# A memory-attention and spatial-gating kernel whose steps are issued in two newly written orders

## The chip, the cores and the metric

The kernel runs on one core of a Trainium2 chip. The time is in device microseconds (us), from the start of the program on the chip to its end; the median of several runs is compared. A profiled execution gives in addition the span of its instructions and, row by row, when each instruction of each engine began and how long it took. The engines of the core are TensorE (PE in the profile; its weight loads are PEld), VectorE (DVE), ScalarE (ACT), GpSimd (POOL) and SyncE (SP, which issues the transfers).

## The reference

Eight batches, eight heads, 576 positions of 64 numbers per head, 32 memories; the model is 512 wide, the hidden layer 1024.

```
# attention through 32 memories
a = softmax of phi over the 576 positions          # (8, 8, 576, 32)
k_m = einsum('bhsm,bhsd->bhmd', a, k)              # keys of the memories
v_m = einsum('bhsm,bhsd->bhmd', a, v)
attn = softmax(q @ k_m^T / 8, over the 32 memories)
x = attn @ v_m                                     # (8, 576, 512) with the heads side by side
# gated layer
h = relu(x @ w_in)                                 # w_in 512 x 1024
u, v = h[..., :512], h[..., 512:]
v_n = (v - mean(v)) / sqrt(var(v) + 1e-6)          # over the last axis
v_s = einsum('ts,bsd->btd', w_spatial, v_n) + b_spatial[None, :, None]
out = (u * v_s) @ w_out                            # w_out 512 x 512
```

w_in and w_out reach the chip as 64-bit floats; all else is float32.

## The kernel before

**The work.** Each batch passes through nine kinds of steps, each named by a letter.

- P: phi of one batch is loaded, its maximum over the positions taken (maxima `half` and `mx`, L319 to L325 on VectorE; a transpose through TensorE to `mt`, L341 on VectorE, and back to `mb`), subtracted (L349) and the exponential taken (ScalarE); then its sums `es` (again L319 to L325, on GpSimd unless the list `ON_VECTOR` names them).
- K: k and v are loaded; TensorE forms the memories' keys and values (L375), the sums give `den` (L397, L398), and small transposes give `kT` and `vT`.
- Q: q is loaded and transposed (batch 0 on TensorE, the others on VectorE).
- S: scores on TensorE, four transposes by VectorE into `sm` (L503), then the softmax over the memories: L509 (maximum), L512 (subtraction), an exponential on ScalarE, L517 (sum), L519 and L520 (reciprocal), L522 (product). After transposes to `aT` the result is split in a high part `ah` (ScalarE) and a low part `al` (L543).
- M0, M1: v_m times the two halves of w_in, so that x itself is never formed; split in `mh` and `ml` (L166).
- V0 to V4: for 128 positions each, the v half (L591), its relu, mean and variance and normalized form, split in `vh` and `vl` (L618).
- U0 to U3: 128 columns each of the u half (L640).
- G0 to G3: the spatial mixture of 128 columns into `ps` (L678), the product `g` of u and `ps` (L689 on VectorE), split in `gh` and `gl` for the first 512 positions and in `grh` and `grl` for the last 64 (casts on ScalarE, L702 on VectorE).
- O0 to O3: 128 positions of the output (`po`, L718). The first half of each reads `gh` and `gl` of two products g, the second half of the other two. O4 does the last 64 positions of two batches at once.

Large products are made of three TensorE products (high by high, high by low, low by high).

**The weights.** Further letters prepare the weights, once. D loads w_in in eight pieces of 512 KB (`raw`, L178). E and L decode the two halves of its columns from 64-bit words to `win_sb`: for each of two row halves, L187 and L193 (VectorE, exponent and fraction), L203, L205 and L208 (ScalarE), L210 (VectorE), then an addition (L216 on GpSimd or L218 on VectorE) and a multiplication (L226 on GpSimd or L223 on VectorE). `ON_VECTOR` says which of them VectorE takes. X0 to X3 do the same for w_out (`raw_out`), and split it in `woh` and `wol` (L251). W loads w_spatial (`w_sb`, `w_rem`) and the bias (`b_sb`); T0 to T4 transpose w_spatial on TensorE and split it in `wth` and `wtl` (L166, where VectorE does it).

**What sets the order.** Each step is a generator, and each token of a text advances one of them by one part. The text `START` runs the preparation and batch 0; the text `PLAN` is run for each of batches 1 to 7. A token `G2` advances the step G2 of the current batch, `S'` the scores of the next batch, `P''` the phi step of the one after it, and `*3` repeats the token. The schedule is manual for all five engines: on each, the instructions stand in the order in which the tokens issued them, and an engine waits at each instruction for its inputs and buffers, with all that stands behind. Waits between engines are worked out from the data; a buffer that is used again makes its next writer wait for its last reader.

```
        for kind, n, ahead in tokens(START):
            step(kind, n, ahead)
        for b in range(1, B):
            for at, (kind, n, ahead) in enumerate(steps):      # steps = the tokens of PLAN
                key = kind, n, b + ahead
                while b + ahead < B and done.get(key, 0) < upto[at]:
                    step(*key)
```

Of the kernel before, what the change touches and what calls it, by code (L numbers as in the profile page):

```python
# [23 lines left out]


START = """
    P*6 W D0 P*4 T1 P D1 B D1 E0 T2*2 D0 T2 D0 P*3 L0 T2 P T1 L0 T1 T2 L0 D0 L1 E0 T1 L0 T1 L1*2
    K E0*2 L0 T1 T2 L1 E0 K W*2 E0 L0 Q E0 T2 W L1 D1 T0 W D1 K E0 T1 K L1 T4 L0 L1 K L1 K Q K
    L0 K*2 T0 E1 T4 E1 T4 K*3 Q P' T4 Q K' Q*6 P'*2 Q*2 S K' E1 S P' S T0 P' T4 S P' M0 E1 T4 S
    E1 P'*2 S T4 M0 X0 M0 E1 T0*3 P' M0 T3 S M0 S P' T3 E1 M0 E1 P' M0 T3 M1 S*2 X1 T0 M1*2 T3  # L30
    P' M1 K' S T3 P' S*2 M1 S P'*2 Q' S T3 M1 K' S Q' U1 M1 T3 S K' U0 S K' X0 K'*2 S K' X1 K'
    X0*3 X1 X0 X1*2 V0 V1 X1 U1 V1 U0 V3 X0 B K' V0 X0 U1 X1*2 V1 U2 X1 U0 X1 V0 U3 X1 X0 P'' X0
    V1 Q'*2 U2 V3 V0 V2 K' Q' V1 X2 V1 V0 V3 V1 X0 U3 U2 V0*2 Q' V2*2 U3 V4*2 G0 P'' V3 V4 G1 S'
    V3 V2*2 S' V4 S' V3 S' G1 S' V2*2 V4 X3 V4 V3 V4 G0 M1' M0'*2 X2 G1 P'' V4 G0 M1' M0' P'' G1
    M0' M1' X2 X3 M1' X3 X2 K'' X2*2 P'' M0' G1 G0*2 M1' P'' M1' X2 G3 X3 G1 G2 P'' M0' X2 G3 X3
    G0 S' P'' G0 X3 G2 S' G3 G1*3 X2 M0' M1' G2 S' G3 X3*3 G2 X2 G0*2 P'' G3 G2 G3 Q'' P'' X2 X3
    G2 S' O1 O0 G3 G2 O3 P'' S'*3 X3 G3 O2 O1 O0 S' G2 O1 K'' O3 O1 O2 S'*2 O0 S' P'' O3 G2 O0
    S'*3 O3 G3 O2 P'' O2 P''*2
"""

PLAN = """
    U0 P'*3 K' P' V1 V0 U0 K' U0 K' V2 U2 V0 V1*3 U1 V2 V0 V2 V0 V4 U1 V1 V0 V2 K' Q' P'' V1 U1
    V3 U3 Q' U2 V1 V4*2 K' V2 P'' K'*2 P'' V3 P'' K' P'' V3 V4 K' K'' U3 K' S' U2 U3 V2 V4 S' V3
    S' V3 S'*2 G0 V4 G1 P'' M0' Q'' P'' M1' M0' S' V3 V2 S' M1'*2 G0 V4 G1 G0 V3 S' G1 V4 G0 P''
    M1' S' M0' Q G1 G0 M1' G0 S' G1 S' M1' K'' P'' G0 S' Q'' G1 G0*2 M0' G2 G3 P'' G2 S' G3 G1*3
    G2 G3 G2*3 M1' G3 O3 G2 S' G3 S'*2 O0 G3 S' O1 G3 O0 S' G3 P'' M0' S' O3 O0 G2 O0 G3 O1 O3
    M0' O3 O4 G2 Q'' O2 M0' O1 O4 O1 V0' O2 O4*2 Q'' O2 V0' O2
"""

ON_VECTOR = set(  # L50
# [760 lines left out]
```

## Time and profile before

| | |
|---|---|
| median of 3 runs | 432.1 us (431.6 to 432.11) |
| span of the profiled execution | 429.2 us |
| TensorE, products | 399.7 us busy (93%), 3844 instructions |
| TensorE, weight loads | 335.9 us (78%) |
| VectorE | 292.5 us (68%), 536 |
| ScalarE | 228.3 us (53%), 438 |
| GpSimd | 81.7 us (19%), 154 |
| transfers | 50.69 MB, 118 GB/s on average |
| costliest lines of the chain that ended last | L678 29%, L718 23%, L591 14%, L640 12%, all TensorE |

The profiled execution's time is its span and what lies around it; the median of the runs is 2.9 us above that span. The page cuts the span in 40 slices of 10.7 us. TensorE's busy digits begin with 3176799 and are 9 from the sixth slice to the last but one; TensorE's clock is at 9 tenths or more in all slices but the fifth, where it is 6. So two stretches can be told apart: a head of some 50 us, in which weights arrive and are decoded, and a long stretch in which TensorE is always busy. In rows of single instructions, the first number is the start in us, the second the duration; then come engine, line, operation, output and inputs with partitions x elements and type, and in brackets how long the engine had idled just before and what ended that. For a group of rows that are alike (x2), the start is that of the first, and the duration covers the group.

### The profile page before, as it was taken

What the parts mean: (1) busy time and instruction counts of PE and PEld (TensorE: products, weight loads), DVE (VectorE), ACT (ScalarE), POOL (GpSimd) and SP (SyncE); (2) the same over time, 40 slices, a digit from 0 to 9 for tenths busy, and PEclk for the clock granted to TensorE, in tenths of its full rate; (3) what the DMA queues carried; (4) which work ended last, traced back from release to release, by engine and by line L of the source; (5) the groups of instructions that cost most, each with busy time, mean ns of one, the idle gap of its engine ahead of it and who ended that gap; (6) DMA issues with size and microseconds to landing.
All of it is one profiled execution on the core that took longest, in us unless ns stands there. A gap on an engine that the chain in (4) does not pass through costs nothing.

```text
span 429.2 us, 9278 instructions
## 1 busy us (share of the span) xinstructions
PE 399.7 (93%) x3844; PEld 335.9 (78%) x3844; DVE 292.5 (68%) x536; ACT 228.3 (53%) x438; POOL 81.7 (19%) x154
## 2 busy tenths in 40 slices
PE   3176799999999999999999999999999999999996
PEld 2063487988798887988798887988798888988984
DVE  3699999994997358953897168955897069824420
ACT  2657697654845277245835176245825276337422
POOL 1344353332300031023200030003200040005000
PEclk9999699999999999999999999999999999999999
DMA  8989639217960369014941279025911200020003
GB/s 291 401 296 323 78 99 225 108 48 178 224 93 25 100 197 185 8 73 141 240 34 43 83 210 178 0 76 185 199 30 58 67 2 0 2 98 2 0 2 121
DMA packets 85790, 50.69 MB, mean 118 GB/s; under 512 B 66226, under 2 KB 70322, under 8 KB 85748
## 3 DMA queue, kind: packets, MB, share of 16 engines
q1 hardware_dynamic: 85748, 50.10, 45.3%
q8 instruction: 30, 0.49, 0.5%
q14 instruction: 12, 0.10, 0.1%
HBM read 40.65 MB, written 9.44 MB: 117 GB/s over the span
## 4 chain that ended last, share of the span: by engine, by line
PE 89%; DVE 4%; DMA 3%; ACT 2%; issue 1%; SPq 0%; ACTq 0%; DVEq 0%
PE ps L678 29%; PE po L718 23%; PE pv L591 14%; PE pu L640 12%; PE kvm L375 4%; PE mp L561 4%; PE sc L492 2%; DMA raw<-in_moe_w_in_dram 2%; DMA w_rem<-in_moe_w_spatial_dram 2%; DVE win_sb L218 1%; DVE power L210 1%; DVE sm L512 1%; ACT raw L208 1%; ACT qT L445 0%; DVE g L689 0%
## 5 line engine op out<-in xcount | busy, mean ns | idle before, releaser
L598 DVE BATCH_NORM_STATS2 st<-vr 128x6 f32<-128x512 f32 (+1 forms) x40 | 27.4, 686 | 46.6 <-ACT vr L595 46.6
L678 PE MATMUL ps<-wth,vh 128*128 128x288 f32 x256 | 57.8, 307 | 0.1
L603 POOL TENSOR_SCALAR rs<-mv 128x1 f32<-128x1 f32 (+1 forms) x40 | 11.6, 291 | 236.1 <-DVE mv L600 232.1
L700 ACT CAST gh<-g 128x512 fp32r<-128x512 f32 x32 | 19.9, 621 | 67.9 <-DVE g L689 67.9
L678 PE MATMUL ps<-wtl,vh 128*128 128x288 f32 x256 | 54.9, 296 | 0.0
L678 PE MATMUL ps<-wth,vl 128*128 128x288 f32 x256 | 54.7, 295 | 0.0
L718 PE MATMUL po<-woh,gh 128*128 128x512 f32 x128 | 50.5, 394 | 0.0
L718 PE MATMUL po<-wol,gh 128*128 128x512 f32 x128 | 50.4, 394 | 0.0
L718 PE MATMUL po<-woh,gl 128*128 128x512 f32 x128 | 50.3, 393 | 0.0
L678 PEld LDWEIGHTS ps<-wth,vh 128*128 128x128 f32 x256 | 40.6, 188 | 11.0 <-issue 5.5
L724 ACT COPY o<-po 128x512 f32<-128x512 f32 x36 | 21.1, 587 | 51.5 <-PE po L718 51.5
L678 PEld LDWEIGHTS ps<-wtl,vh 128*128 128x128 f32 x256 | 41.3, 188 | 0.0
L678 PEld LDWEIGHTS ps<-wth,vl 128*128 128x128 f32 x256 | 41.3, 188 | 0.0
L613 ACT ACTIVATE vr<-vr,sh,rs 128x512 f32<-128x512 f32 (+1 forms) x40 | 32.4, 815 | 2.6 <-POOL sh L608 2.3
L591 PE MATMUL pv<-mh,ah 128*128 128x512 f32 (+1 forms) x80 | 32.9, 411 | 0.0
L649 ACT ACTIVATE u<-pu 128x576 f32<-128x576 f32 x32 | 20.2, 659 | 21.8 <-PE pu L640 21.5
L595 ACT ACTIVATE vr<-pv 128x512 f32<-128x512 f32 (+1 forms) x40 | 23.8, 595 | 14.6 <-PE pv L591 14.6
L591 PE MATMUL pv<-ml,ah 128*128 128x512 f32 (+1 forms) x80 | 31.6, 395 | 0.0
L591 PE MATMUL pv<-mh,al 128*128 128x512 f32 (+1 forms) x80 | 31.6, 395 | 0.0
L689 DVE TENSOR_TENSOR g<-u,ps 128x576 f32<-128x576 f32 x32 | 23.9, 750 | 10.8 <-PE ps L678 10.5
L718 PEld LDWEIGHTS po<-woh,gl 128*128 128x128 f32 x128 | 24.0, 188 | 5.7
L718 PEld LDWEIGHTS po<-woh,gh 128*128 128x128 f32 x128 | 24.0, 188 | 5.2
(150 smaller groups left out, 872.2 us busy)
## 6 DMA issues: line engine op xcount, KB each, us to landing
kv_sb<-in_k_dram SPq DMA_DIRECT2D x8, 1152.0 KB, 6.9
kv_sb<-in_v_dram SPq DMA_DIRECT2D x8, 1152.0 KB, 8.9
out_dram<-o SPq DMA_DIRECT2D x32, 256.0 KB, 2.0
q_sb<-in_q_dram SPq DMA_DIRECT2D x28, 288.0 KB, 6.5
phi_sb<-in_phi_dram SPq DMA_DIRECT2D x8, 576.0 KB, 4.1
raw<-in_moe_w_in_dram SPq DMA_DIRECT2D x8, 512.0 KB, 8.1
raw_out<-in_moe_w_out_dram SPq DMA_DIRECT2D x4, 512.0 KB, 3.6
w_sb<-in_moe_w_spatial_dram SPq DMA_DIRECT2D x1, 1152.0 KB, 6.8
```

Source lines behind the costliest of these rows:

```text
L375: nc.tensor.matmul(kvm[r][32 * j : 32 * j + 32], phi_sb[halves[r], j, i, :], kv_sb[halves[r], j, :, i * D : (i + 1) * D], start=(i == 0), ...
L591: nc.tensor.matmul(pv, x[:, r, cs], m[:, r, DM:DFF], start=(n == 0), stop=(n == 5))
L595: nc.scalar.activation(vr, pv, AF.Relu)
L598: nc.vector.bn_stats(st6, vr)
L613: nc.scalar.activation(vr, vr, AF.Identity, bias=sh, scale=rs)
L640: nc.tensor.matmul(pu[:, hf, 0:HALF], m[:, r, cs], a[:, r, hf * HALF : (hf + 1) * HALF], start=(n == 0), stop=(n == 5),)
L649: nc.scalar.activation(u[:, dt, :].rearrange("p (a s) -> p a s", a=2), pu[:, :, 0:HALF], AF.Relu)
L678: nc.tensor.matmul(ps[:, hf, 0:HALF], a, w[:, hf * HALF : (hf + 1) * HALF], start=(n == 0), stop=(n == len(ops) - 1),)
L689: nc.vector.tensor_tensor(g.rearrange("p (a s) -> p a s", a=2), u[:, dt, :].rearrange("p (a s) -> p a s", a=2), ps[:, :, 0:HALF], op=ALU.mult,
L700: nc.scalar.copy(hi, x)
L718: nc.tensor.matmul(po, a, w, start=(n == 0), stop=(n == 11))
L724: nc.scalar.copy(o, po)
```

## The change

The texts `START` and `PLAN` are written anew. All steps, their operations, the shapes, the buffers and `ON_VECTOR` stay. Of the diff two lines of each text tell the form; what moves on the engines is shown below.

```
 START = """
-    P*6 W D0 P*4 T1 P D1 B D1 E0 T2*2 D0 T2 D0 P*3 L0 T2 P T1 L0 T1 T2 L0 D0 L1 E0 T1 L0 T1 L1*2
+    P D0 P*3 D0 P D1 P*2 D1 P*2 L0 P L0*2 W L0 T2 L0 P D0 T1 W D0 L0 T1 L0 Q L0 E0 T2 L1 E0 K*2
...
 PLAN = """
-    U0 P'*3 K' P' V1 V0 U0 K' U0 K' V2 U2 V0 V1*3 U1 V2 V0 V2 V0 V4 U1 V1 V0 V2 K' Q' P'' V1 U1
+    U2 P' V1 V0*2 U0 P' V1 P' V1 U2 V0 V1 V2 U2 V1 V4 V0*2 K' P' V1 K' V2 U0 K' V1 U3 Q K' V4 V2
...
```

**Loads at the start.** SyncE issues the transfers in this order from the start of the program; here is that piece as a difference, - before and + now.

```order
 L330 DMA phi_sb<-in_phi_dram 128x4x288
+L178 DMA raw<-in_moe_w_in_dram 128x1024 x4
 L260 DMA w_sb<-in_moe_w_spatial_dram 128x4x576
 L261 DMA w_rem<-in_moe_w_spatial_dram 64x576
 L263 DMA b_sb<-in_moe_b_spatial_dram 1x576 x2
-L178 DMA raw<-in_moe_w_in_dram 128x1024 x6
+L178 DMA raw<-in_moe_w_in_dram 128x1024 x2
+L434 DMA q_all<-in_q_dram 128x4x576
 L363 DMA kv_sb<-in_k_dram 128x4x576
 L363 DMA kv_sb<-in_v_dram 128x4x576
-L434 DMA q_all<-in_q_dram 128x4x576
 L178 DMA raw<-in_moe_w_in_dram 128x1024 x2
```

Four pieces of w_in now come directly behind phi and ahead of w_spatial, two more behind it, and q ahead of k and v; the last two pieces stay last.

**GpSimd in the head.** GpSimd's rows from the clearing of the bias buffer to the last decoding of w_in, as a difference; `es` are the sums of batch 0's phi, and the rows L216 and L226 decode w_in in halves of a tile.

```order
 L134 MEMSET t_90 64x512
 L259 MEMSET b_sb 64x576
+L226 TENSOR_TENSOR win_sb<-win_sb,power 128x512 x2
 L319 TENSOR_TENSOR half<-phi_sb 128x512
 L321 TENSOR_TENSOR half<-half 128x4x64
 L323 TENSOR_TENSOR es<-half 128x128
 L325 TENSOR_TENSOR es<-es,phi_sb 128x128
-L226 TENSOR_TENSOR win_sb<-win_sb,power 128x512 x2
 L216 TENSOR_TENSOR win_sb<-win_sb,raw 128x512 x2
 L226 TENSOR_TENSOR win_sb<-win_sb,power 128x512 x2
```

The first multiplication moves ahead of the sums; the order of the rest stays.

**VectorE at the scores of batch 0.** `sm` takes the four score transposes, `mx` and `half` are the maxima of batch 1's phi, and L210 joins sign and exponent of weights still to be decoded. Before:

```order
L319 TENSOR_TENSOR half<-phi_sb 128x512
L321 TENSOR_TENSOR half<-half 128x4x64
L503 STREAM_TRANSPOSE sm<-sc_0_0_361 128x288
L323 TENSOR_TENSOR mx<-half 128x128
L503 STREAM_TRANSPOSE sm<-sc_0_1_362 128x288
L325 TENSOR_TENSOR mx<-mx,phi_sb 128x128
L503 STREAM_TRANSPOSE sm<-sc_1_0_363 128x288
L503 STREAM_TRANSPOSE sm<-sc_1_1_364 128x288
L341 TENSOR_REDUCE cm<-mt_391 128x2
L509 TENSOR_REDUCE rmx<-sm 128x36
L210 SCALAR_TENSOR_TENSOR power<-raw,power 128x1024
```

And now, at the same place:

```order
L503 STREAM_TRANSPOSE sm<-sc_0_1_347 128x288
L193 TENSOR_SCALAR raw_out<-raw_out 128x512
L210 SCALAR_TENSOR_TENSOR power<-raw,power 128x1024
L319 TENSOR_TENSOR half<-phi_sb 128x512
L321 TENSOR_TENSOR half<-half 128x4x64
L323 TENSOR_TENSOR mx<-half 128x128
L325 TENSOR_TENSOR mx<-mx,phi_sb 128x128
L503 STREAM_TRANSPOSE sm<-sc_1_0_348 128x288
L503 STREAM_TRANSPOSE sm<-sc_1_1_349 128x288
L341 TENSOR_REDUCE cm<-mt_418 128x2
L509 TENSOR_REDUCE rmx<-sm 128x36
```

The decoding of the last w_in rows (L210) and the first of w_out (`raw_out`) moved ahead of the maxima, which now stand in one block between the second and the third score transpose, where they had alternated with the first three.

**VectorE around the fourth product g of batch 0.** `mp` are the products with w_in for batch 1 and `ml` their low parts; `rsum` and the second `sm` belong to the softmax of batch 1, and `phi_sb` with `mb` to phi of batch 2. Before:

```order
L166 TENSOR_TENSOR ml<-mp_0_1_870,mh 128x512
L166 TENSOR_TENSOR ml<-mp_1_1_860,mh 128x512
L210 SCALAR_TENSOR_TENSOR power<-raw_out,power 128x512
L702 TENSOR_TENSOR grl<-g,grh 128x64
L689 TENSOR_TENSOR g<-u,ps_3_938 128x576
L689 TENSOR_TENSOR g<-u,ps_2_947 128x576
L349 TENSOR_TENSOR phi_sb<-phi_sb,mb_1025 128x1152
L517 TENSOR_REDUCE rsum<-sm 128x36
L702 TENSOR_TENSOR gl<-g,gh 128x512 x2
L519 TENSOR_SCALAR rsum<-rsum 128x36
L520 RECIPROCAL rsum<-rsum 128x36
L522 TENSOR_TENSOR sm<-sm,rsum 128x1152
```

And now:

```order
L517 TENSOR_REDUCE rsum<-sm 128x36
L689 TENSOR_TENSOR g<-u,ps_3_946 128x576
L349 TENSOR_TENSOR phi_sb<-phi_sb,mb_960 128x1152
L519 TENSOR_SCALAR rsum<-rsum 128x36
L520 RECIPROCAL rsum<-rsum 128x36
L166 TENSOR_TENSOR ml<-mp_0_1_868,mh 128x512
L166 TENSOR_TENSOR ml<-mp_1_1_854,mh 128x512
L522 TENSOR_TENSOR sm<-sm,rsum 128x1152
L702 TENSOR_TENSOR gl<-g,gh 128x512
L702 TENSOR_TENSOR grl<-g,grh 128x64
L689 TENSOR_TENSOR g<-u,ps_2_988 128x576
```

The row L689 that reads `ps_2` makes the fourth product. The subtraction L349, the softmax rows L517, L519, L520 and L522 and one `gl` stood behind it and now stand ahead of it.

More of the change, by code (lines that the diff above doesn't have):

```diff
@@ L26 @@
 START = """
-    P*6 W D0 P*4 T1 P D1 B D1 E0 T2*2 D0 T2 D0 P*3 L0 T2 P T1 L0 T1 T2 L0 D0 L1 E0 T1 L0 T1 L1*2
[L28 to L38, printed above, removed]
+    P D0 P*3 D0 P D1 P*2 D1 P*2 L0 P L0*2 W L0 T2 L0 P D0 T1 W D0 L0 T1 L0 Q L0 E0 T2 L1 E0 K*2
@@ new lines @@
+    E0 P Q D1 E0 D1 L1 Q T2 L1 Q L1 E0*2 Q*2 T1*2 Q L1 P T2 P L1 Q P Q E0 T1 E0 Q T2 Q L1 X0 X1
+    L1 K W Q K T1 K E1 B E1 K T2 K*3 X0 T1 K P' K E1 K K' S X0 S X1 S E1*2 X1 T3 Q' T3 X1 M0 T3
+    E1 T2 P' M0 X1 P' M0 T3 P' T0 P' T0 S P' E1 S T3 P' M0 W T3 S T0*2 K' P' T3 P' M0*2 T0 S*2 P'
+    S E1 S X0 S X0*2 W T0 M1 P' M1 Q' M0 S*2 M1*2 P' M1 S T0 K' P' S T4 M1 P' S*2 P' X0 U0 M1 T4
+    S*2 K' T4 V0 K'*2 X0 V0*2 B K' X0 T4 U0 P'' V1 U0 U2 X1 Q' X1 K'*2 U2 V1 U2 V1 V2 V0 Q' V1 K'
+    V4 V0 Q' X0 U1 T4 P'' V0 P'' U1 X1 V0 V1 X1 X0 K' V4 V3 Q' K' V4 U1 U3 V2 U3 V1*2 V2 V4 X1 V3
@@ L39 @@
+    U3 X1 P'' S'*2 V4 X2 T4 V2 P'' G0 V3 T4 S' V2 G1 G0 P'' V3 V4 V2 S' V3 X2 M1' S' V3 P'' M0'
+    X2*2 M1' V2 X3 M0' M1' V3 X2*2 S' G1 M0' X3 V4 X3 V4 X2 G0 G1 P'' M0' G0 G1 G0 M0' X3 G0 M1'
+    G1 M1' S' G3*2 G1 P'' M1' K'' X3*2 X2 G1 M0' G1 G3 S' G1 G3 X3 G0 G2 O3 S' G2 X2 G3 G2 P'' X2
+    S' M0' G3 X3 Q'' M1' S' X3 P'' G0 X3 G2 O1 G3 X2 G0 G2 S' X3 G2 O0 S' G2 O2 S' G2 O1*2 O2*2
+    G2 O1 P'' K'' S' P'' O0 S' G3 P''*2 O0 O3 S' O0 S' O3 O2 S' O3 G3
 """
 PLAN = """
-    U0 P'*3 K' P' V1 V0 U0 K' U0 K' V2 U2 V0 V1*3 U1 V2 V0 V2 V0 V4 U1 V1 V0 V2 K' Q' P'' V1 U1
@@ L43 @@
[L43 to L47, printed above, removed]
+    U2 P' V1 V0*2 U0 P' V1 P' V1 U2 V0 V1 V2 U2 V1 V4 V0*2 K' P' V1 K' V2 U0 K' V1 U3 Q K' V4 V2
@@ L48 @@
+    Q' U3 V4 U0 U3 V3 U1 V2 K' U1 V2 V4 Q' K'*2 G0 K'*2 V3*2 K' S' V3 S' V4 S' U1 G0 V2 S' V4 G1
+    K'' S' P'' S' V3 S' K'' M0' V3 M0' M1' V2 M1' V4 G1 G0 P'' G1 S' V4 M1' V3 P'' G1*2 G0 M0' G2
+    M1' G2*3 G1 M1' G0 G3 G0 S' P''*2 G3 S' Q'' G3 S' G0 G1 G0 G3 G1*2 G0 S' M0' G2 O0 S' G2 M0'
+    G3 S' O1 M0' G2 G3 M0' M1' G3 S' P'' O1 P'' O0 S' O1 O2 M1' P'' S'*2 G2*2 O2 P'' O2 G3 P'' O1
+    Q'' O4 O0 O2 O3 G3 O4*2 S' O0 O4 O3 Q''*2 P'' V0' O3*2 V0'
 """
```

## The prediction

> **What bounds the kernel now.** I read the page's first two parts, then busy time by stretch, then the rows of each engine in order of time.
>
> ```profile
> PE 399.7 (93%) x3844; PEld 335.9 (78%) x3844; DVE 292.5 (68%) x536; ACT 228.3 (53%) x438; POOL 81.7 (19%) x154
> 10.00:20.00 10.00, 2.11 (x6) 0.95 (x4) 5.61 (x8) 6.21 (x10) 3.57 (x4) 1.00 1.04 403
> 41.10:44.30 3.20, 0.00 (x0) 0.00 (x0) 3.20 (x3) 1.65 (x3) 3.20 (x3) 0.94 0.90 114
> 44.30:47.10 2.80, 2.68 (x17) 0.51 (x17) 2.73 (x4) 1.64 (x3) 2.09 (x2) 0.50 1.07 139
> 47.30:50.70 3.40, 2.92 (x81) 2.22 (x81) 3.31 (x9) 2.57 (x6) 0.00 (x0) 0.50 0.66 57
> 52.50:90.80 38.30, 38.28 (x289) 32.82 (x284) 35.72 (x68) 29.42 (x56) 18.42 (x23) 1.00 0.49 121
> 90.80:425.30 334.50, 334.38 (x3111) 286.03 (x3109) 216.74 (x413) 167.22 (x321) 44.94 (x109) 1.00 0.39 92
> ```
>
> In the rows by stretch the columns are the stretch, its length, busy time of PE, PEld, DVE, ACT and POOL, the granted clock, the DMA share and GB/s. From 52.5 us TensorE does not pause: 38.28 of 38.30 us, then 334.38 of 334.50. Before that it idles. So the time is TensorE's fixed work plus what it idles in the head, and a new order of the steady part can only lose there. Until 90.8 VectorE is nearly as full (35.72 of 38.30), so it is the engine to account for.
>
> One place allows an exact comparison.
>
> ```profile
> 85.92 1.40 DVE L689 TENSOR_TENSOR g<-u,ps 128x576 f32<-128x576 f32 x2
> 86.69 0.62 ACT L700 CAST gh<-g 128x512 fp32r<-128x512 f32 x1 [1.47 <-DVE g L689]
> 90.80 0.39 PE L718 MATMUL po<-woh,gh 128*128 128x512 f32 x1
> ```
>
> The row at 90.80 is the 25th projection matmul of batch 0, the first that reads the second half of gh. The two orders have the same matmuls ahead of it (all of K0, K1, M0, M1, V0, U0, S1, G0 and the first halves of O0 to O3) and the same behind it. Behind it TensorE has 334.5 us of work without a pause, in either order, unless the new steady part stalls. The change is therefore worth (start of this matmul in the new order) − 90.80. It needs the fourth product g (here ending at 87.32) and its cast.
>
> **The new order's transfers.** phi lands at 4.83 (first DVE row below). Then come 2.10 MB of w_in, 1.33 of w_spatial, 1.05 of w_in, and 1.18 each of q, k and v: 8.0 MB at 403 GB/s (row of 10 to 20 us) is 19.9 us, so v lands near 24.7. TensorE's memories K0 began at 24.64 in this profile, held by transposes of w_spatial. So K0 does not move; q now lands first, its transposes fill TensorE's idle time, and scores can follow K0 at about 30.3 instead of 34.0. That 3.7 us is the change's real gain.
>
> **VectorE against GpSimd.** The gain has to pass VectorE, and its rows beside GpSimd's decoding are long.
>
> ```profile
> 27.77 4.41 POOL L226 TENSOR_TENSOR win_sb<-win_sb,power 128x512 f32<-128x512 f32 x2 [12.83 <-DVE win_sb L218]
> 24.07 1.22 DVE L223 TENSOR_TENSOR win_sb<-win_sb,power 128x1024 f32<-128x1024 f32 x1
> 29.08 1.96 DVE L223 TENSOR_TENSOR win_sb<-win_sb,power 128x1024 f32<-128x1024 f32 x1
> 30.96 1.76 DVE L187 TENSOR_SCALAR power<-raw 128x1024 int32<-128x1024 int32 x1
> 37.88 3.51 POOL L216 TENSOR_TENSOR win_sb<-win_sb,raw 128x512 f32<-128x512 f32 x2 [5.71 <-ACT raw L208]
> 38.52 1.73 DVE L210 SCALAR_TENSOR_TENSOR power<-raw,power 128x1024 int32<-128x1024 int32 x1
> 40.17 2.44 DVE L512 TENSOR_TENSOR sm<-sm,rmx 128x1152 f32<-128x1152 f32 x1
> 41.36 3.62 POOL L226 TENSOR_TENSOR win_sb<-win_sb,power 128x512 f32<-128x512 f32 x2
> 45.23 1.28 DVE L519 TENSOR_SCALAR rsum<-rsum 128x36 f32<-128x36 f32 x1
> 78.99 1.34 DVE L509 TENSOR_REDUCE rmx<-sm 128x36 f32<-128x1152 f32 x1
> 80.67 1.44 POOL L216 TENSOR_TENSOR raw_out<-raw_out 128x512 f32<-128x512 f32 x1 [0.34 <-ACT raw_out L208]
> 80.85 2.47 DVE L512 TENSOR_TENSOR sm<-sm,rmx 128x1152 f32<-128x1152 f32 x1
> ```
>
> L223 takes 1.22 us alone and 1.96 beside GpSimd, and ends when GpSimd's first multiplication (27.77, half of 4.41) has ended plus 1.1 of its own. L512 takes 2.44 and 2.47 beside GpSimd; without it the equally large L522 takes 1.36 (below), a wait of 1.1. Reductions (L509, 1.34) don't wait. The reading that fits them all: an operation of VectorE with two SBUF inputs, or a TENSOR_SCALAR from SBUF, and one of GpSimd take turns, each waiting for the other's whole instruction. In this profile the waits ahead of the fourth g come to about 6.2: 0.74 (L223), 1.1 (L187), 0.5 (L210), 1.1 (L519), 1.1 twice (L512), 0.6 at 12 to 15 us.
>
> The new order puts four short dependent operations (the maxima of phi, L319 to L325) straight beside GpSimd's four half-tiles of the last w_in decoding.
>
> ```profile
> 33.86 0.67 DVE L319 TENSOR_TENSOR half<-phi_sb 128x512 f32<-128x512 f32 x1
> 34.56 0.42 DVE L321 TENSOR_TENSOR half<-half 128x256 f32<-128x256 f32 x1
> 36.16 0.25 DVE L325 TENSOR_TENSOR mx<-mx,phi_sb 128x128 f32<-128x128 f32 x1
> 36.33 0.84 DVE L503 STREAM_TRANSPOSE sm<-sc 128x288 f32<-128x288 f32 x2
> 50.94 0.76 DVE L543 TENSOR_TENSOR al<-aT,ah 128x576 fp32r<-128x576 f32 x1 [0.29 <-ACT ah L541]
> ```
>
> By my sum GpSimd starts L216 at 33.7 (ScalarE's L203, L205 and L208 behind den), VectorE L319 at 33.8. All four lose a turn of 1.1 us: 1.7 becomes 6.2, so L325 ends near 40 and the last two score transposes behind it begin at 40.1 rather than near 35.6; here they began at 36.33. The rest of the softmax (L509, L512, exp, L517, L522, transposes, ah, al) follows at 11.3 us, so the first al ends at 51.4, against 51.70 here. The 3.7 us are gone. A milder case: where VectorE's next instruction is already due, GpSimd waits (row at 56.71, below), L319 then escapes, and the four waits are three.
>
> ```profile
> 56.71 2.22 POOL L226 TENSOR_TENSOR raw_out<-raw_out,power 128x512 f32<-128x512 f32 x1 [10.24 <-issue]
> 57.10 0.68 DVE L218 SCALAR_TENSOR_TENSOR raw_out<-raw_out 128x512 f32<-128x512 f32 x1
> ```
>
> The Trainium skill, page "SBUF — State Buffer", section "Who interferes with whom", says that whichever of the two issues first holds the shared ports for its whole instruction and the other fully blocks. By it L216, 0.1 us ahead, keeps all four waits; by the row just shown it is three, and the sum would be 1.1 us lower.
>
> **What stands ahead of the fourth g.** Counted over the rows of the two orders, five VectorE operations of batch 1's softmax, one of phi, and one gl move ahead of it; nothing moves behind.
>
> ```profile
> 87.24 1.34 DVE L349 TENSOR_TENSOR phi_sb<-phi_sb,mb 128x1152 f32<-128x1152 f32 x1
> 88.51 1.34 DVE L517 TENSOR_REDUCE rsum<-sm 128x36 f32<-128x1152 f32 x1
> 89.77 1.28 DVE L702 TENSOR_TENSOR gl<-g,gh 128x512 fp32r<-128x512 f32 x2
> 91.17 0.38 DVE L520 RECIPROCAL rsum<-rsum 128x36 f32<-128x36 f32 x1
> 91.59 1.36 DVE L522 TENSOR_TENSOR sm<-sm,rsum 128x1152 f32<-128x1152 f32 x1
> ```
>
> By start-to-start distance: L349 1.26, L517 1.26, one gl 0.6, L519 and L520 0.5, L522 1.26: +4.9 us.
>
> Waits for GpSimd ahead of it in the new order: 2.4 at 15 to 21 (L187, two L193, L210 beside the sums of phi, L319 to L325 on GpSimd), 4.5 at 33 to 40, then about 1.1 each for L321 beside L251, L210 beside L216, a grl beside the second L216, and a gl beside L251, and 0.7 in small ones: 12.0, so +5.8.
>
> VectorE's own idling falls.
>
> ```profile
> 4.83 0.69 DVE L319 TENSOR_TENSOR half<-phi_sb 128x512 f32<-128x512 f32 x1 [4.83 <-DMA phi_sb<-in_phi_dram]
> 8.44 1.35 DVE L349 TENSOR_TENSOR phi_sb<-phi_sb,mb 128x1152 f32<-128x1152 f32 x1 [0.90 <-PE mb L347]
> 12.65 1.98 DVE L187 TENSOR_SCALAR power<-raw 128x1024 int32<-128x1024 int32 x2 [2.85 <-DMA raw<-in_moe_w_in_dram]
> 16.45 0.69 DVE L187 TENSOR_SCALAR power<-raw 128x1024 int32<-128x1024 int32 x1 [0.96 <-DMA raw<-in_moe_w_in_dram]
> 19.67 2.36 DVE L210 SCALAR_TENSOR_TENSOR power<-raw,power 128x1024 int32<-128x1024 int32 x2 [0.73 <-ACT power L205]
> 22.81 1.23 DVE L218 SCALAR_TENSOR_TENSOR win_sb<-win_sb,raw 128x1024 f32<-128x1024 f32 x1 [0.77 <-ACT raw L208]
> ```
>
> With w_in behind phi, 0.90 + 2.85 + 0.96 + 0.73 + 0.77 = 6.2 us of idling go, and one of 2.9 comes (the third pair of w_in now lands behind w_spatial, near 15.8). About 1.2 us of waits under 0.6 go as well, since VectorE is late: −4.5. Six more dependent operations in direct succession lose some 0.1 each: +0.6.
>
> Fourth g: 87.32 + 4.9 + 5.8 − 4.5 + 0.6 = 94.1 (93.0 with three waits). Cast and hand-over, 0.03 + 0.62 + 0.1 (row at 86.69): the 25th matmul at 94.9.
>
> **The clock.** Here TensorE did nothing from 41.1 to 44.3, and its clock was 0.50 until 50.7. In the new order it has nothing from about 36.2 to 40.6 (its next row waits for the maxima), and little until 43.5. I expect a half-clock stretch again, but with TensorE's K1, T4, U0 and V0 in it, which VectorE waits for. What it adds lies between 0 (no stretch, or over by 47) and 3.0 (until 54); I take 1.2, nearer to its end at 50.7 as here. The Trainium skill, "TensorE: Matmul & The Clock Gate", section on the HAM clock gate, gives a window of 3.4 us without work to halve the clock and one of busy work to restore it; this profile's 3.2 us agree, and by its free-running window the end could fall anywhere from 50.7 to 54.
>
> Sum: 96.1 − 90.80 = +5.3. The profiled span is 429.2, the median of the runs 432.1, so 2.9 lie around it; I add the difference to the median: 437.3, rounded to 437.2.
>
> **TensorE's own floor.** Without any wait for g, TensorE would reach the 25th matmul at about 90.7: the first U0 starts near 51.1 instead of 52.5, but 1.3 us of K1 are then still to do. So VectorE's lateness counts in full from there.
>
> **Costed at nothing.** The steady order: every instruction stays, and by the rows' durations no matmul waits over 0.25 us; VectorE's slack there (216.74 busy of 334.5) covers it. If that cover failed by 0.2 us a batch, seven batches would add 1.4. The SP queue's reordered loads have landed 10 us or more before use.
>
> **Rivals.**
> - The turns fall the other way, GpSimd giving way to VectorE as at 57.10, everywhere. Then 4.5 + 5.1 of the waits vanish, al ends near 47, TensorE runs from there and is ahead: about −3.2, 428.9, faster. It decides if L321 to L325 run at their bare 0.3 to 0.4. Against it: L223, L512 (twice) and L519 all waited. 8%.
> - TensorE hides VectorE's lateness: the fourth g ends before 90. That needs 4 of the 6.8 us to be misjudged. 432.1. 7%.
> - Worse: half clock until 54 and all four waits, or a stall in each steady batch: +6.5 to +8.5, near 439.6. 12%.
> - The forecast, 434 to 439: 73%.
>
> No change that can be told is within 0.2% (0.9 us). Faster 0.09 (the first rival and a little of the second), same 0.06, slower 0.85. The range leaves out the first rival, half of the second and the end of the third: 432.4 to 440.4.
>
> **What will show it.** Right: L321, L323 and L325 near 35 to 40 us at 1.2 to 1.6 each; the last two L503 at about 40; clock 0.50 between 40 and 51 or later; the fourth g near 94 to 96; TensorE waiting for L689 or L700 between 76 and 97, some 4 us in all. Wrong: short maxima rows, the 25th projection matmul near 91 or earlier, or pauses of TensorE behind it.

## The result, and the profile after

The changed kernel takes 437.09 us (median of 4 runs, 436.02 to 437.62) against 432.11 of the kernel before: a ratio of 1.012, with a 95% interval of 1.0103 to 1.0136. The forecast was 437.2. As the account below shows, the sum came out right because wrong terms of it cancelled.

The profiled execution has a span of 435.5 us, 6.3 more than the one before; the medians differ by 5.0. Executions of the kernel before with a span of 429.2 took 431.0 us, so its profiled execution was 1.1 us faster than its median, and that much of the 6.3 is scatter.

The busy times on the page of the changed kernel:

```profile
PE 399.1 (92%) x3844; PEld 334.6 (77%) x3844; DVE 292.7 (67%) x536; ACT 229.3 (53%) x438; POOL 73.4 (17%) x154
```

Stretches of the changed kernel, as in the prediction (start and end, length, busy time of PE, PEld, DVE, ACT and POOL, clock, DMA share, GB/s):

```profile
5.00:10.00 5.00, 0.92 (x2) 0.36 (x2) 3.25 (x7) 1.05 (x2) 0.00 (x0) 1.00 0.92 304
10.00:15.00 5.00, 0.00 (x0) 0.00 (x0) 3.96 (x5) 2.50 (x3) 1.49 (x1) 1.00 1.04 346
15.00:20.00 5.00, 2.75 (x10) 1.79 (x10) 0.74 (x2) 1.69 (x4) 4.16 (x6) 1.00 1.04 367
42.60:49.40 6.80, 4.24 (x22) 1.43 (x22) 6.48 (x9) 4.90 (x10) 0.82 (x1) 0.50 1.08 240
49.40:56.20 6.80, 6.15 (x92) 4.79 (x93) 6.07 (x15) 3.80 (x9) 0.00 (x0) 0.50 0.35 48
...
0.00:55.00 55.00, 26.26 (x370) 16.54 (x371) 40.01 (x62) 31.15 (x59) 14.55 (x22) 0.89 0.89 271
55.00:98.75 43.75, 41.17 (x365) 34.32 (x363) 39.82 (x68) 28.71 (x55) 18.92 (x23) 0.99 0.30 79
```

And one of the kernel before, which the prediction did not show:

```profile
0.00:52.50 52.50, 27.05 (x452) 17.08 (x452) 39.99 (x57) 31.04 (x60) 18.30 (x22) 0.93 0.89 284
```

The fourth g, its cast, and the 25th projection matmul of batch 0, row by row:

```profile
97.29 0.75 DVE L689 TENSOR_TENSOR g<-u,ps 128x576 f32<-128x576 f32 x1
98.08 0.62 ACT L700 CAST gh<-g 128x512 fp32r<-128x512 f32 x1 [3.76 <-DVE g L689]
98.75 0.50 PE L718 MATMUL po<-woh,gh 128*128 128x512 f32 x1 [1.16 <-ACT gh L700]
```

The matmul starts at 98.75, 7.95 us later than before. From its start to the start of the last matmul of the program it was 334.08 us and is now 332.45. So the head lost 7.95 and the steady part gained 1.63: together 6.3, the whole difference of the spans.

TensorE was busy for 27.05 + 38.28 = 65.33 us ahead of that matmul and idle for 25.5; now it is busy for 26.26 + 41.17 = 67.43 and idle for 31.3. The matmuls ahead of it are the same. So 5.85 of the 7.95 are idle time, and 2.1 are the same matmuls at a lower clock: the half-clock stretch runs from 42.6 to 56.2, where it was 43.9 to 50.7. What TensorE waited for until the 25th matmul (sum, times, longest):

```profile
PE wt L287 <- DMA w_sb<-in_moe_w_spatial_dram: 7.6, 1, 7.6
PE mt L338 <- DVE mx L325: 6.7, 1, 6.7
PE mt L338 <- DVE sm L503: 4.1, 1, 4.1
PE tq L443 <- DMA q_all<-in_q_dram: 3.6, 1, 3.6
PE mp L159 <- ACT mh L570: 2.2, 1, 2.2
PE mb L347 <- ACT cmb L344: 1.6, 2, 0.9
PE kvm L375 <- DMA kv_sb<-in_v_dram: 1.5, 1, 1.5
PE po L718 <- ACT gh L700: 1.2, 1, 1.2
PE tk L415 <- ACT kmn L402: 1.1, 1, 1.1
PE ps L678 <- DVE g L689: 0.9, 1, 0.9
PE po L718 <- DVE gl L702: 0.5, 1, 0.5
```

Three groups of these are to be seen. Among the early ones, the loads (7.6 + 3.6 + 1.5) take the place of other waits: ahead of the first scores TensorE idles 21.2 us, where it was 20.0. In the middle stand two large waits: 4.1 at 38.5, for a score transpose that stands behind the maxima on VectorE, and 2.2 at 47.8, for a cast on ScalarE. At the end are 2.6 us of waits for g and its parts, where there were none before. Up to the first U0 the idle time is 28.7 us for 25.4, so 3.3 of the 5.85 arise ahead of U0 and 2.6 behind it.

The maxima on VectorE, and, in the second fence, GpSimd beside them:

```profile
36.33 1.79 DVE L319 TENSOR_TENSOR half<-phi_sb 128x512 f32<-128x512 f32 x1
38.15 1.39 DVE L321 TENSOR_TENSOR half<-half 128x256 f32<-128x256 f32 x1
39.65 1.17 DVE L323 TENSOR_TENSOR mx<-half 128x128 f32<-128x128 f32 x1
40.85 1.23 DVE L325 TENSOR_TENSOR mx<-mx,phi_sb 128x128 f32<-128x128 f32 x1
```

```profile
36.27 2.99 POOL L216 TENSOR_TENSOR win_sb<-win_sb,raw 128x512 f32<-128x512 f32 x2 [16.88 <-ACT raw L208]
39.22 2.72 POOL L226 TENSOR_TENSOR win_sb<-win_sb,power 128x512 f32<-128x512 f32 x2
```

All four lost a turn to one of GpSimd's four half-tiles, as forecast, though 2.5 us later than forecast; the last ends at 42.1, not at 40. Where VectorE idled ahead of the fourth g (two of its larger gaps, in brackets):

```profile
19.26 0.69 DVE L187 TENSOR_SCALAR power<-raw 128x1024 int32<-128x1024 int32 x1 [5.30 <-DMA raw<-in_moe_w_in_dram]
25.05 1.23 DVE L210 SCALAR_TENSOR_TENSOR power<-raw,power 128x1024 int32<-128x1024 int32 x1 [2.16 <-ACT power L205]
```

### The profile page after: what moved, and what is told of

Same layout as the page of the kernel before. It is cut to its first block, busy times and chain, and to the rows that moved or that the text cites. A ratio compares the mean times of both kernels' runs of the same rounds, so it can differ in the third digit from the quotient of the medians.

```text
span 435.5 us, 9286 instructions
## 1 busy us (share of the span) xinstructions
PE 399.1 (92%) x3844; PEld 334.6 (77%) x3844; DVE 292.7 (67%) x536; ACT 229.3 (53%) x438; POOL 73.4 (17%) x154
## 4 chain that ended last, share of the span: by engine, by line
PE 73%; DVE 15%; ACT 5%; DMA 5%; issue 1%; SPq 0%; POOL 0%; DVEq 0%; ACTq 0%
PE po L718 22%; PE ps L678 21%; PE pv L591 12%; PE pu L640 11%; PE kvm L375 4%; DMA q_all<-in_q_dram 3%; DMA raw<-in_moe_w_in_dram 2%; DVE sm L503 1%; PE mp L561 1%; DVE sm L512 1%; DVE rmx L509 1%; DVE vl L618 1%; DVE st L598 1%; PE sc L492 1%; DVE power L210 1%
## 5 line engine op out<-in xcount | busy, mean ns | idle before, releaser
L678 PE MATMUL ps<-wth,vh 128*128 128x288 f32 x256 | 56.9, 304 | 1.0 <-DVE g L689 0.9
L700 ACT CAST gh<-g 128x512 fp32r<-128x512 f32 x32 | 19.9, 621 | 70.2 <-DVE g L689 70.2
L718 PE MATMUL po<-woh,gh 128*128 128x512 f32 x128 | 51.1, 399 | 1.2 <-ACT gh L700 1.2
L724 ACT COPY o<-po 128x512 f32<-128x512 f32 x36 | 21.2, 588 | 56.9 <-PE po L718 48.7
L603 POOL TENSOR_SCALAR rs<-mv 128x1 f32<-128x1 f32 (+1 forms) x40 | 9.1, 228 | 241.5 <-DVE mv L600 205.4
L678 PEld LDWEIGHTS ps<-wth,vh 128*128 128x128 f32 x256 | 40.6, 188 | 10.2 <-issue 8.7
L618 DVE TENSOR_TENSOR vl<-vr,vh 128x512 fp32r<-128x512 f32 x32 | 21.8, 685 | 22.8 <-ACT vh L616 22.6
L591 PE MATMUL pv<-mh,ah 128*128 128x512 f32 (+1 forms) x80 | 31.8, 397 | 0.0
L689 DVE TENSOR_TENSOR g<-u,ps 128x576 f32<-128x576 f32 x32 | 23.7, 742 | 11.2 <-PE ps L678 11.1
L640 PE MATMUL pu<-ah,mh 128*128 128x288 f32 x128 | 28.6, 304 | 0.9 <-issue 0.9
```

Source lines behind the costliest of these rows:

```text
L591: nc.tensor.matmul(pv, x[:, r, cs], m[:, r, DM:DFF], start=(n == 0), stop=(n == 5))
L618: nc.vector.tensor_tensor(vl[:, st, :], vr, vh[:, st, :].bitcast(F32), op=ALU.subtract)
L640: nc.tensor.matmul(pu[:, hf, 0:HALF], m[:, r, cs], a[:, r, hf * HALF : (hf + 1) * HALF], start=(n == 0), stop=(n == 5),)
L678: nc.tensor.matmul(ps[:, hf, 0:HALF], a, w[:, hf * HALF : (hf + 1) * HALF], start=(n == 0), stop=(n == len(ops) - 1),)
L689: nc.vector.tensor_tensor(g.rearrange("p (a s) -> p a s", a=2), u[:, dt, :].rearrange("p (a s) -> p a s", a=2), ps[:, :, 0:HALF], op=ALU.mult,
L700: nc.scalar.copy(hi, x)
```

## The experiments

Each kernel is compared with the kernel before on the same chip, and given as a ratio with its 95% interval. The changed kernel's own is 1.012 (1.0103 to 1.0136), so differences to it under 0.2% tell nothing. Diffs are of the step lists; dots stand for tokens that stay.

**New head, old steady order.** START as changed, PLAN as before.

> The new START with the old PLAN. First theory: the new steady order is worth 1.6 us on TensorE (from the 25th projection matmul to the last it takes 332.45 us after and 334.08 before), and the head costs the rest, so this gives 437.1 + 1.6 = 438.7. Second theory: all of the change lies in the head and the 1.6 us are scatter between two profiled executions: 437.1.

Measured: 440.54 us, ratio 1.021 (1.0191 to 1.0228). It is slower than either theory said. The old steady order does not fit behind the new head: one wait of 2.4 us comes up in its first batch, and a half-clock stretch of 3.4 us follows. A row of TensorE:

```profile
106.61 1.46 PE L375 MATMUL kvm<-kv_sb,phi_sb 64*32 64x128 f32 x80 [2.44 <-issue]
```

From the 25th matmul on it takes 337.72 us. The two halves of the change are thus not independent in this direction.

This run also gives a second view of the new head. `START` is that of the changed kernel, and TensorE idles 31.3 us ahead of the 25th matmul in both; but the half-clock stretch here is one of 10.2 us, not 13.7.

```profile
42.90:53.10 10.20, 6.84 (x102) 3.28 (x102) 9.99 (x15) 7.75 (x16) 0.51 (x1) 0.50 0.92 176
```

```profile
97.33 0.51 PE L718 MATMUL po<-woh,gh 128*128 128x512 f32 x1 [1.18 <-ACT gh L700]
```

The 25th matmul starts at 97.33 for 98.75: 3.4 us less at half clock bring 1.4. So starts in two profiled executions can be compared only where their half-clock stretches are alike, and this execution, with U0 at 54.15, is the measure for those below that had 10.2 us.

**Old head, new steady order.** START as before, PLAN as changed.

> The old START with the new PLAN. First theory (the steady order saves 1.6 us on TensorE by itself): 432.1 - 1.6 = 430.5, with the 25th projection matmul still at 90.8 and 332.5 us behind it. Second theory (steady order without effect): 432.1. Third (the new steady order needs the progress of the new head, and stalls here): 433 or more, with pauses of TensorE behind 91 us.

Measured: 430.58 us, ratio 0.9973 (0.9963 to 0.9982); 25th matmul at 91.0, 332.79 us behind it. The first theory holds: this half of the change is a gain. It would be larger without one new pause of TensorE, 1.3 us at 251.9 (a U step); the changed kernel has one too, of 0.9.

**One token of the old steady order.** What in the new order gains? Its two halves of the next batch's memory products stand back to back.

```
 PLAN
-    U0 P'*3 K' P' V1 V0 U0 K' U0 K' V2 ...
+    U0 P'*4 V1 V0 U0 K'*2 U0 K' V2 ...
```

> The kernel before, with one token of PLAN moved: the two halves of the next batch's memory products (64x32 blocks, L375) stand back to back, as in the new steady order, in place of P', V1, V0 and U0 between them. First theory (the new steady order's 1.3 to 1.6 us come from fewer changes between kinds of matmuls; a break in the L375 block costs some 0.22 us each): six or seven breaks fewer, 430.3 to 430.9 against 431.7 for the kernel before on this chip. Second theory (the gain lies elsewhere in the new order): 431.7.

Measured: 429.79 us, ratio 0.9965 (0.9953 to 0.9978), with 332.01 us from the 25th matmul on. This single token brings all that the new steady order brings, and the kernel is the fastest of this study. And the reverse:

```
 PLAN (the changed one, behind the old START)
-    ... V1 U2 V0 V1 V2 U2 V1 V4 V0*2 K' P' V1 K' V2 ...
+    ... V1 U2 K' V0 V1 V2 U2 V1 V4 V0*2 P' V1 K' V2 ...
```

> The old START with the new PLAN in which the two halves of the next batch's memory products are taken apart again (the first half two V steps earlier on TensorE, 12 matmuls between them). First theory (the whole gain of the new steady order is that the halves stand together): the 1.1 to 1.3 us are lost, ratio 0.999 to 1.001, and from the 25th projection matmul to the last TensorE takes 334 to 335 us in place of 332.8. Second theory (other parts of the order gain too): 0.997 stays.

Measured: 431.25 us, ratio 0.9997 (0.9988 to 1.0005), 333.88 us. The gain is gone, though no row shows a wait. The price stands in the starts. In one batch of the kernel before:

```profile
147.69 1.37 PE L375 MATMUL kvm<-kv_sb,phi_sb 64*32 64x128 f32 x80
148.99 0.50 PE L591 MATMUL pv<-mh,ah 128*128 128x512 f32 x1
149.32 0.40 PE L591 MATMUL pv<-ml,ah 128*128 128x512 f32 x1
```

The matmul behind the block starts 0.20 us after the block's last product, where the products follow each other at 0.014, and its successor another 0.33 later, where 0.23 is usual. The block's first product starts 0.22 after the matmul ahead of it, where 0.13 is usual. That is some 0.38 us for each break. The steady part agrees: the halves together bring 334.08 - 332.01 = 2.07 us in six batches, 0.34 each; taking them apart costs 333.88 - 332.79 = 1.09, and 2.4 or 0.40 each if the pause of 1.3 us is taken off, which the new steady order has and this run has not. So TensorE pays at the changes between 64x32 blocks and 128x128 matmuls.

**The last decoding on VectorE.** ON_VECTOR with E1.add and E1.mul added.

> The changed kernel, with the addition and multiplication of the last decoding of w_in taken from GpSimd and given to VectorE (1.22 + 1.23 us more for VectorE, GpSimd idle between 20 and 45 us). First theory (the four maxima rows are long because each waits for a GpSimd instruction): L319 to L325 take 0.67, 0.42, 0.28 and 0.27 instead of 1.79, 1.39, 1.17 and 1.23, L325 ends near 38.1 instead of 42.1, the first al comes 4.0 - 2.45 = 1.5 us earlier, and the time is 435.6 to 436.5. Second theory (they are long for another reason, such as their chain of dependence or the transfers in flight): the rows stay long, the 2.45 us come on top, 438.5 to 439.5.

Measured: 436.76 us, ratio 1.0117 (1.0103 to 1.0132). The maxima, with GpSimd empty:

```profile
36.63 0.68 DVE L319 TENSOR_TENSOR half<-phi_sb 128x512 f32<-128x512 f32 x1
37.35 0.43 DVE L321 TENSOR_TENSOR half<-half 128x256 f32<-128x256 f32 x1
37.88 0.29 DVE L323 TENSOR_TENSOR mx<-half 128x128 f32<-128x128 f32 x1
38.20 0.29 DVE L325 TENSOR_TENSOR mx<-mx,phi_sb 128x128 f32<-128x128 f32 x1
```

The same four rows at the same place take 1.7 us, not 5.6. That GpSimd made them long is shown. The time did not move. VectorE's two additional operations (1.18 and 1.22) and what followed left the first al only 0.64 us earlier (52.11 for 52.75), and TensorE, which no longer waits 4.1 us behind the maxima, waits for the second of these operations instead:

```profile
46.98 1.93 PE L561 MATMUL mp<-win_sb,vT 64*32 64x512 f32 x8 [2.90 <-DVE win_sb L223]
```

**The maxima ahead of GpSimd's decoding.** No work added; only the order of START is changed.

```
 START (token by token)
-    S X1 S E1*2 X1 T3 Q' T3 X1 M0 T3 E1 T2 P' M0 X1 ...
+    S*2 E1*2 T3 Q' T3 M0 T3 T2 P' M0 ...
```

The E1 taken out stands behind S's L512, two X1 behind the first al and two behind the second.

> The changed kernel, with the four maxima of batch 1's phi moved ahead of GpSimd's last decoding (they come right behind the second score transpose, at 34.9 us; the decoding rows L210, L187 and L193 that stood there follow later). No work is added. First theory (waits for GpSimd delay VectorE and the delay is passed on): the maxima take 0.7, 0.4, 0.3 and 0.3 us, the first al comes 3.5 us earlier, near 49.2, the first U0 3 us earlier, and the time is 433 to 435. Second theory (VectorE is not what sets U0; TensorE's own queue in front of it is: K1, T4 and a wait for ScalarE at half clock): al comes earlier, U0 by less than 1 us, time 436 to 437.

Measured: 434.52 us, ratio 1.0084 (1.0071 to 1.0097); first al at 50.76, U0 at 52.50, 25th matmul at 95.68. Two of the four still met GpSimd:

```profile
34.72 0.69 DVE L319 TENSOR_TENSOR half<-phi_sb 128x512 f32<-128x512 f32 x1 [0.43 <-DMA phi_sb<-in_phi_dram]
35.45 0.42 DVE L321 TENSOR_TENSOR half<-half 128x256 f32<-128x256 f32 x1
35.98 1.36 DVE L323 TENSOR_TENSOR mx<-half 128x128 f32<-128x128 f32 x1
37.38 1.26 DVE L325 TENSOR_TENSOR mx<-mx,phi_sb 128x128 f32<-128x128 f32 x1
```

The first theory holds in kind, at about half its size: VectorE's lateness here was passed on to U0 and to the time. TensorE's idle time ahead of the 25th matmul fell from 31.3 to 28.4. The half-clock stretch was 10.2 us; beside the execution of the new head with an equal stretch, U0 and the 25th matmul come 1.65 us earlier, much as the ratios have it (0.36%, 1.6 us). That waits for GpSimd alone did it is not shown: L325 ends at 38.64 for 42.08, of which 1.8 us are turns not lost, and 1.6 come of the decoding rows that now stand behind the maxima.

**Five operations and a gl behind the fourth g.** S' and P'' tokens of START (L517, L349, L519, L520, L522) and one G3 token moved behind G2's product and cast.

> The changed kernel, with the operations that had moved ahead of the fourth g (L517, L349, L519, L520, L522 and one gl) put behind it and behind its cast. First theory (by now TensorE is itself nearly late enough: from the first U0 at 55.0 it has 41.2 us of work, and only its waits of 1.16 and 0.46 us for gh and gl hang on these rows): the fourth g ends near 93, the 25th projection matmul starts 1.2 to 1.6 us earlier, 435.5 to 435.9. Second theory (the recorded one, VectorE's lateness counts in full): 4.9 us earlier, 432.2.

Measured: 437.57 us, ratio 1.0134 (1.0118 to 1.015). The fourth g ends at 93.57, 4.5 earlier; the 25th matmul starts at 98.29, 0.5 earlier. VectorE's row, and two of TensorE's:

```profile
92.82 0.75 DVE L689 TENSOR_TENSOR g<-u,ps 128x576 f32<-128x576 f32 x1 [1.70 <-PE ps L678]
```

```profile
96.82 0.47 PE L718 MATMUL po<-woh,gh 128*128 128x512 f32 x1 [1.25 <-DVE phi_sb L349]
100.04 0.50 PE L718 MATMUL po<-woh,gl 128*128 128x512 f32 x1 [1.12 <-DVE gl L702]
```

Now VectorE waits for TensorE (1.70). The move made waits of its own, 2.4 us together: the trace names L349 as what TensorE waited for with 1.25 (it is the last reader of `mb`, whose PSUM bank a later tile takes), and the late gl with 1.12, behind the 25th matmul. So neither theory's time came. Without the 1.25, the 25th matmul would start near 97.0, an estimate from these rows: 1.7 us earlier than in the changed kernel, close to the first theory's 1.2 to 1.6, and far from 4.9. The prediction's reading that VectorE's lateness counts in full falls: in this execution, whose half-clock stretch was 13.7 us too, TensorE with its other waits is not ready before 97.0, where the prediction had 90.7.

**ScalarE's decoding of w_out.** X0's tokens for L205 and L208 moved behind M1's casts and the first ah.

> The changed kernel, with ScalarE's two decoding rows of w_out (L205 and L208 of X0, 0.70 and 0.65 us at 47.1) moved behind the casts of M1 and the first ah. First theory (TensorE's wait of 2.2 us at 47.8 is for the cast mh, which stands behind these rows on ScalarE): the wait falls to about 1.0, U0 starts 1 to 1.2 us earlier, and the time falls by about 1 us, to a ratio of 1.009 to 1.010. Second theory (VectorE's order holds the end): no change, 1.012.

Measured: 435.53 us, ratio 1.0091 (1.0078 to 1.0105). The wait:

```profile
48.82 0.79 PE L159 MATMUL mp<-mh,minus 128*128 128x512 f32 x1 [1.17 <-ACT mh L570]
```

The wait falls from 2.21 to 1.17 and the ratio is within the first theory's. U0 starts at 53.69 for 55.02, but most of that is the clock's: the half-clock stretch was 10.2 us, and beside the execution of the new head with an equal one U0 is 0.5 earlier (54.15) and the 25th matmul 0.35 (96.98 for 97.33). That the shorter wait gives the whole gain of the medians, 0.3%, is not shown. **Both moves together**, this one and the maxima:

> The changed kernel with the maxima ahead of GpSimd's last decoding and with ScalarE's w_out rows behind M1's casts. First theory (TensorE's idle time before U0 is the sum of separate waits, and each one that goes is gained): ratio 1.008 for the first move alone, another 1 us for the second, 1.005 to 1.006, with TensorE idle some 27 us ahead of the 25th projection matmul (31.3 in the changed kernel, 25.5 before). Second theory (they share one wait, so the second brings nothing on top): 1.008.

Measured: 434.92 us, ratio 1.0082 (1.0068 to 1.0096). That is the second theory's time, but not its cause. TensorE's wait for mh with the maxima alone, then with both moves:

```profile
48.07 0.80 PE L159 MATMUL mp<-mh,minus 128*128 128x512 f32 x1 [3.32 <-ACT mh L570]
```

```profile
48.00 0.80 PE L159 MATMUL mp<-mh,minus 128*128 128x512 f32 x1 [2.28 <-ACT mh L570]
```

With the maxima early, TensorE reaches the cast earlier and waits longer for it; the second move takes 1.04 off this wait, as it did alone. In this execution it was lost again ahead of the wait, since batch 1's phi came later and VectorE began L319 at 35.87 for 34.72. Why the medians show no second gain stays open.

**TensorE filled.** Eight products that nobody reads, in an unused part of the bank `mb`, behind M1.

> The changed kernel with eight more TensorE products (128x128, into an unused part of a PSUM bank, read by nobody) where TensorE waits for ScalarE from 47.8 to 50.0 us. First theory (the half clock goes on for a second 6.83 us because TensorE was not busy through the end of the first): the half-clock stretch is 6.8 in place of 13.7 us, K1 and T4 in front of U0 take 2.3 us less, U0 starts near 53.3, and the time is 434.5 to 436. Second theory (VectorE sets the end in any case): the stretch is shorter, the time within 0.5 of 437. Third: the stretch stays 13.7 and the time 437.

Measured: 436.05 us (434.81 to 437.71), ratio 1.0121 (1.0102 to 1.014). The stretch:

```profile
44.60:51.40 6.80, 6.53 (x36) 4.43 (x35) 6.63 (x10) 4.89 (x9) 0.00 (x0) 0.50 1.12 162
```

In this execution the long stretch is one of 6.8 us (an earlier one of 3.4, at 34.4, came on top), and U0 starts at 54.06. But the filling took 3.8 us and so ran 1 us past the wait it was to fill. The time did not change beyond the scatter, so this run says nothing on the price of the clock.

That price comes from two pairs. One is the changed kernel and its head with the old steady order, above: 3.4 us at half clock, 1.4 us of time. In the other, the profiled execution of the kernel with the K halves together (its slowest, 431.66) has the same START as the kernel before and the same idle time ahead of the 25th matmul (25.5 in both), but a half-clock stretch of 13.7 us in place of 6.8. Its second half, then the same stretch before:

```profile
50.60:57.40 6.80, 6.80 (x114) 6.07 (x98) 5.36 (x16) 4.59 (x12) 0.00 (x0) 0.50 0.31 89
```

```profile
50.70:57.50 6.80, 6.78 (x117) 5.67 (x110) 6.38 (x17) 4.87 (x12) 0.79 (x1) 1.00 0.30 89
```

Its 25th matmul starts at 93.51 for 90.80: another 6.8 us at half clock, with TensorE busy in them, cost 2.7 us.

**The loads.** Two experiments. In the first, w_in comes in four transfers of 1 MB.

```
-            for j in range(2):
-                rows = slice((2 * n + j) * P, (2 * n + j + 1) * P)
-                nc.sync.dma_start(raw[:, j], w_in[rows, c * 512 : (c + 1) * 512].bitcast(I32))
-                yield
+            rows = slice(2 * n * P, (2 * n + 2) * P)
+            src = w_in[rows, c * 512 : (c + 1) * 512].bitcast(I32)
+            nc.sync.dma_start(raw, src.rearrange("(j p) f -> p j f", j=2))
+            yield
+            yield
```

> The changed kernel with w_in loaded in four transfers of 1 MB in place of eight of 512 KB. SyncE's waits show that each transfer waits for the one issued eight before it; v is issued at 15.9, when w_spatial has landed. First theory (these waits thin out the stream and let later transfers share with v): v is issued near 10, lands near 24 to 25 in place of 28.3, K0, the scores and all behind them come 3 to 3.7 us earlier, and the time is 433.5 to 434.5. Second theory (the bytes set the landing; the waits are hidden): K0 at 28, time 437. Third (K0 and scores come earlier, but VectorE's decoding behind them does not): scores earlier by 3, al by less than 1, time 436 to 437.

Measured: 436.2 us, ratio 1.0119 (1.0106 to 1.0133), K0 at 28.13. The second theory: v was issued at 11.7 in place of 15.9 and K0 did not move. In the second, w_spatial comes ahead of w_in again (the token W moved to the second place of START).

> The changed kernel, with w_spatial and the bias loaded ahead of w_in again, directly behind phi; q, k and v follow in the new order. This undoes the part of the change that its words name first. First theory (the order of these loads decides nothing: K0 waits for v, whose bytes come last in either order, and VectorE's decoding has 5.3 and 2.2 us of waiting at 14 to 25 us to spare): K0 at 28 as before, TensorE's wait of 7.6 us for w_spatial is gone but nothing follows from it, time within 0.5 us of the changed kernel (ratio 1.010 to 1.013 to the kernel before). Second theory (w_in behind phi is worth what the decoding gains): the decoding ends up to 3 us later than 31.0, and the time is 438 to 440.

Measured: 436.2 us, ratio 1.0109 (1.0095 to 1.0123): no loss, and within the scatter no gain. VectorE, then TensorE:

```profile
30.10 0.21 DVE L397 TENSOR_SCALAR den<-kvm 128x1 f32<-128x1 f32 x2
```

```profile
25.56 2.22 PE L375 MATMUL kvm<-kv_sb,phi_sb 64*32 64x128 f32 x143 [0.97 <-DMA kv_sb<-in_v_dram]
31.04 0.73 PE L415 MATMUL tk<-ident,kmn 128*128 128x128 f32 x2 [2.98 <-ACT kmn L402]
```

Here K0 started 2.8 us earlier than in the changed kernel, and TensorE gave 1.9 of it back: den stands on VectorE behind the decoding, which ended at 30.1 (31.0 in the changed kernel). The idle time ahead of the 25th matmul fell to 28.9, but a half-clock stretch of 6.8 us came on top of one of 13.7, and the busy time rose from 67.4 to 68.9. So w_in directly behind phi is worth nothing that these medians show, and K0 was not what the scores waited for.

## Why the prediction was right, and where it was not

**The sign: right. The cause: right in part.** VectorE loses turns to GpSimd in one block, and TensorE, without pause from 52.5 before, is idle longer in the head. The four maxima, the clock of 0.50 past 51 us and the late fourth g were all seen, the maxima and g some 2 us later than stated. TensorE's waits for L689 and L700 came to 2.1 us, not 4. With the maxima moved away, 0.36% of the 1.2% came back. The rival in which GpSimd gives way is out: L321 to L325 took 1.39, 1.17 and 1.23. The Trainium skill, "SBUF — State Buffer", "Who interferes with whom", says that whoever issues first holds the shared ports for its whole instruction; the trace agrees, with L216 at 36.27, 0.06 us ahead of L319, and four turns lost.

**"So K0 does not move": wrong.** It moved from 24.64 to 28.34. The stream ran at 304, 346 and 367 GB/s in the stretches from 5 to 20 us, not at 403, and by the GB/s of the stretches some 0.8 MB of transfers issued behind v arrived ahead of its end. The price was nil, as the run with w_spatial first shows; for the same reason "the change's real gain" of 3.7 us was 1.0. The scores came that much earlier (32.98 for 34.01): VectorE's decoding, ending at 31.0, held them.

**VectorE's idling, −4.5: wrong in sign.** Its gaps ahead of the fourth g sum to 18.9 us, and to 15.1 before: +3.8. I had the third pair of w_in land near 15.8; it was used at 19.26 (5.30 idle). And I left out that ScalarE takes its rows in order: L205 stood behind a copy that waited for q (2.16).

**Waits for GpSimd, +5.8: too large.** The turns lost sum to 3.9 at the maxima, and 1.0 to 1.1 each at L321, L210, a grl and a gl later, as named: 8.2, not 12.0; so +2.0. The 2.4 at 15 to 21 could not occur, since VectorE idled there. With +4.9, +3.8 and +2.0 the fourth g ends at 98.0, as measured; the +0.6 for direct succession finds no place.

**Five operations ahead of the fourth g, +4.9: right for VectorE, wrong for the time.** (The prediction speaks of five operations of the softmax; it sums four and L349, and that is what moved.) Put back, g ends 4.5 earlier, the 25th matmul starts 0.5 earlier and the time does not fall, in part because the move made 2.4 us of waits of its own. "VectorE's lateness counts in full" rested on TensorE's floor at 90.7, and that was the step that failed. TensorE had its own lateness, from its other waits and the half clock: the first U0 came at 55.02, not near 51.1.

**The clock, +1.2 of at most 3.0: too small, and the stretch outlasted its bound.** It ended at 56.2, not by 54. TensorE's busy time for the same matmuls rose by 2.1, and by the price of the two pairs 6.8 us more at half clock are worth some 2.7. Over the heads of all runs the stretches last 3.4, 6.8, 10.2 or 13.7 us. The Trainium skill, "TensorE: Matmul & The Clock Gate", on the HAM clock gate, calls the window of some 3.4 us free-running and its cost variable from run to run; the trace agrees, since one and the same old head had 6.8, 10.2 and 13.7, and the new one 10.2 and 13.7. Two and more such stretches can follow each other, so one of them did not bound the end. Nor did the 3.2 us without work agree with a whole idle window, as the prediction has it: by the 0.94 in that row, the clock halved 0.4 us before the pause ended, after 2.8 us of it.

**The steady order at nothing: wrong, −1.6.** "A new order of the steady part can only lose there" took busy time for needed time. The K halves show it. The cover did fail in one place, a pause of 0.9 us.

So the 25th matmul came at 98.75 where the sum had 96.1. The steady order gave 1.6 back, and the median moved 1.3 less than the profiles. That these two, which the sum did not have, bring 437.1 so near to 437.2 is luck.

**What stays open.** The idle time of +5.85 has several causes (waits of 4.1 for the maxima, 2.2 for ScalarE, 2.6 for g), and the two moves that gained, together, recovered only 0.4% of 1.2%. How the waits hang together is not shown. No run shows which part of the new head costs the rest. What a head without a half-clock stretch would return was not measured, and each run has one profiled execution, so part of the differences between them is the clock's.

## What to carry to other kernels

A busy engine is not at its floor: look for kinds of matmuls that alternate, and try equal ones back to back; here a break cost time that no wait shows. Before costing an engine's lateness in full, add up the other engine's own path to the same point; taking away 4.5 us of lateness moved the time by nothing, in part because the move made new waits. Compare the half-clock stretches of two executions before their starts. Where VectorE's two-input operations run in a dependent chain, place them where GpSimd is quiet, but see first what stands next in the row of waits.

## What the runs showed of the hardware

Breaking a block of 144 small products (64x32) in two, with 128x128 matmuls between, cost some 0.34 to 0.40 us a block (2.07 us over six batches one way, an estimated 2.4 the other), at no visible wait. Half-clock stretches in the heads came as multiples of 3.4 us and differed between the executions of one and the same `START`; 6.8 us of them under a busy TensorE cost 2.7 us, and 3.4 us cost 1.4. A pause of 2.4 us (new head, old steady order) was enough for one to follow.

The operations of VectorE that lost a turn to GpSimd took 0.9 to 1.1 us longer, whatever their own length: 1.79, 1.39, 1.17 and 1.23 us for the four maxima, and 0.68, 0.43, 0.29 and 0.29 with GpSimd empty.
